# A new written order for the long convolution and the start of the MLP in a two-layer convolution and MLP kernel

## The chip, the cores and the metric

The kernel runs on one core of one Trainium2 chip. The metric is device time in microseconds (us), the median of three runs. A core has five engines that each take their own instructions in order and wait for each other through semaphores: TensorE (PE, matmuls), VectorE (DVE), ScalarE (ACT), GpSimd (POOL) and SyncE (SP, which here issues nearly all DMAs). DMAs are transfers between memory and on-chip SBUF, or within SBUF. Matmuls write PSUM, from which DVE or ACT copies the result to SBUF.

## The reference, cut to what matters

```python
x = A_q
x = x + A(LN(x), k, v, shift_k, ssm_k, ssm_D)
x = x + B(LN(x), w1, b1, w2, b2)
x = x + A(LN(x), k, v, shift_k, ssm_k, ssm_D)
x = x + B(LN(x), w1, b1, w2, b2)

def A(q, k, v, ...):            # S = 2048 tokens, D = 512 channels
    kv = shift(k, 4 taps) * v
    y = irfft(rfft(kv padded) * rfft(ssm_k padded))[:S] + kv * ssm_D
    return q * y
def B(x, w1, b1, w2, b2):       # F = 1376
    return gelu(LN(x) @ w1 + b1) @ w2 + b2
```

The result y of the convolution depends on k, v and the filters alone, so it is computed once and used in both layers.

## The kernel before: tiles, stages and what sets the order

The convolution is a two-stage transform, all of it matmuls with tables. Channels go in four chunks of 128 (cc 0 to 3), the 32 outer frequencies in four groups of eight (j 0 to 3). Every bit of work is a named **piece**:

- `lk`, `lv`, `lK`, `lx0`, `lF`, `lW`, `lM` are loads (k, v, the filter ssm_k in four quarters, the first tokens of q, tables). `kT` transposes k, `kv` is the 4-tap shift as matmuls (L513), `kvm` multiplies it by v on DVE out of PSUM (L521). The last chunk's taps run on POOL (`kg`, `ka`, `kgm`, L445 to L456).
- `KS` and `K2` transform the filter (L384, L394). `sa`, `sb` are eight DMAs that write its real and imaginary halves swapped (L401).
- `U..S`, `U..T` are the first stage for the signal (L302, L334 or a transposing DMA, L281).
- `X{cc}{j}` is the second stage, eight matmuls of 128 columns (L548), copied from PSUM to a buffer `xb`. `T{cc}{j}` multiplies it with the filter's spectrum, both operands in SBUF (L563), by DVE or by POOL. `V{cc}{j}` is the way back, 16 matmuls (L571), copied from PSUM to a buffer `ZT`. `T33` and `V33` come in two halves, a and b.
- `Z{cc}{g}` are transposing DMAs for chunks 0 to 2 (L619), `TD{g}` are transposes of chunk 3 on PE (L607), `Y{g}` is the last matmul stage for a group of four token tiles (L639).
- `s00`, `s01`, `s02` are the layer norm of the first tokens. `g0`, `h0`, `p0`, `b0`, `LT` are the gate, the statistics, the norm and the transposes of the first token group, `M` the first product of its MLP (L695) with its gelu (L703). `w1` to `w4` load the MLP's weights. `wm` are matmuls whose results nobody reads.

Nothing decides the order at run time or by a planner. A long string `ORDER` (L18) is written out by hand as words such as `T00.G` or `X01.P21`: the piece, a letter for the engine (P, D for DVE, A for ACT, G for POOL, S for SP) and the numbers of the buffers that it takes (`P` alone: which of four PSUM buffers; for X the second number is the `xb` buffer, of nine; three `ZT` buffers in the same way). `write` (L91 to L100) emits the pieces in just this order, under manual scheduling, so each engine gets its words in the string's order. For an evacuation of PSUM the letter chooses ACT or DVE (L208), for a `T` piece DVE or POOL (L559).

After the string the program continues in plain loops: second product of the MLP for the first group (L766), then seven more groups (L732, L766), with the second layer's norm and gate between them.

Of the kernel before, what the change touches and what calls it, by code (L numbers as in the profile page):

```python
# [15 lines left out]


ORDER = """  # L18
lk0.S lSK.S wm0.P0 bS.P2 bSK.P1 lk1.S bSe.A lb1.S kT1.P0 lF.S kT0.P2 bB.P3 dg1.D dg0.D kT0e.D bSKe.A kT1e.A lh1.S kT3.P1 kT2.P0 lh113.S dg2.A lv0.S kv01.P2 bBe.D kT3e.D lK11.S kvm01.D lv1.S kv00.P1 lK01.S kv20.P2 kvm00.D lK10.S kvm20.D kd6.P1 kT2e.A U1S0.P00 U1S0e.D kv02.P3 kd6e.A KS71.P2 KS71e.A KS70.P1 KS61.P0 lK00.S KS70e.A kvm02.D U1S1.P3 KS61e.D U1S1e.D kv03.P2 kd2.P0 U0S0.P11 kd2e.A U0S0e.A kvm03.D KS60.P3 U0S2.P0 U0S2e.A KS60e.D U2S0.P22 KS21.P1 kd4.P3 kd4e.D U0S3.P0 U2S0e.A U0S3e.A KS51.P3 KS40.P2 KS40e.A KS21e.D KS51e.D KS20.P1 KS30.P0 wm1.P2 KS30e.A KS20e.D U2S1.P3 U2S1e.A KS50.P2 kd0.P0 kd0e.D KS31.P1 KS50e.A KS00.P0 KS00e.A KS31e.D KS01.P3 KS11.P2 KS41.P1 KS10.P0 lx0.S KS01e.D KS11e.A U1S2.P3 U0S1.P2 KS41e.D KS10e.A kg0.G kg1.G ka1.G kg2.G ka2.G kg3.G ka3.G U0S1e.A wm2.P1 U1S2e.D lH.S lW.S K24.P0 K24e.A K23.P1 K23e.A K29.P2 K27.P3 K27e.A K29e.A kv21.P0 K21.P1 s00.D kvm21.D K22.P3 K20.P2 K21e.A K22e.D K26.P0 K25.P1 K25e.D K20e.A K28.P3 K211.P2 K211e.D K26e.A K210.P0 K28e.A U2S2.P1 lM.S K210e.A K213.P3 K213e.A U2S2e.D K214.P2 K212.P0 K212e.D s01.G kgm.G K214e.A K215.P1 sa0.S K215e.A U0T0.P3 U0T0e.D U1S3.P2 sb0.S U2S3.P0 U1S3e.A U0T1.P1 X00.P30 X01.P21 U2S3e.A X00e.A T00.G U0T1e.D X01e.A U2T0.P0 U3S0.P11 U3S0e.A U2T1.P3 U3S3.P2 U3S3e.A U2T0e.D X20.P02 X20e.A T20.G U2T1e.D U3S1.P1 U3S1e.D U3S2.P3 U1T0.P2 X23.P00 sa2.S U1T1.P1 sb1.S U1T0e.D U3S2e.A U1T1e.D sa3.S X11.P33 X23e.A X22.P24 sa1.S sb3.S X11e.A X21.P05 X21e.A sb2.S U3T0.S lx.S U3T1.S X03.P16 X22e.D X03e.A T23.D ly.S X12.P37 X02.P22 X13.P08 X12e.A V00.P1 T21.D X10.P30 X13e.A V20.P00 X02e.A V00e.A X10e.A T01.D T22.D V23.P2 V20e.A V22.P1 V22e.A T03.D V03.P3 V03e.A V23e.A V21.P0 T02.D T10.D V02.P1 V01.P3 V02e.A V21e.D T12.D T13.D V01e.A Z21.S Z20.S X30.P00 X32.P22 X32e.A X30e.D V10.P11 V13.P3 V10e.A V13e.A X31.P28 X31e.A V12.P0 T11.D Z00.S Z01.S T30.D T32.D V11.P1 V12e.A T31.D V11e.A X33.P33 Z22.S Z10.S Z11.S V30.P22 V32.P0 X33e.A w1.S V32e.A T33a.D T33b.D V30e.A V31.P1 V31e.D V33a.P3 V33ae.A V33b.P0 V33be.A TD0a.P1 TD0ae.A s02.D TD0b.P3 TD0be.D Y00.P0 Y00e.A Y01.P1 TD3.P3 g00.D h00.D p00.G Z02.S Y01e.A TD1.P2 TD2.P0 TD3e.A TD1e.A TD2e.A Y02.P3 g01.D Y10.P2 b00.D LT0.P1 Y02e.A LT0e.A Z12.S Y12.P0 h01.D p01.G g02.D Y10e.A Y12e.A M0b.P3 M0be.A M0a.P1 b01.D h02.D LT1.P0 M0ae.A LT1e.D Z03.S Y20.P3 M1b.P0 p02.G b02.D LT2.P2 M1be.A LT2e.A M1a.P1 M2a.P0 Y20e.A M1ae.A M2ae.A M2c.P3 M2ce.A M2b.P2 M2be.A Y22.P0 w3.S w4.S Z13.S Z23.S Y32.P3 Y30.P1 LG1.D Y32e.A w2.S Y30e.A Y22e.A
"""  # L20
NA, NB = 32, 64

# [824 lines left out]
```

## Time and profile before

| what | us |
|---|---|
| median of three runs | 248.03 |
| lowest and highest run | 246.64, 249.02 |
| span of the profiled execution, first to last instruction | 245.9 |
| PE busy | 236.2 |
| DVE busy | 169.9 |
| ACT busy | 137.0 |
| POOL busy | 62.5 |

The page gives no time of the profiled execution but its span; the span lies 2.1 us below the median of the runs and 0.7 us below the lowest. Times in views are us from the start of the span. In a timeline a row has start, length, engine, line, operation, output and input, and a count; in the chain of waits a row has start, length and what the chain went through. "SPq" is the SP queue issuing a DMA. The convolution and the MLP's begin take the span's first 99.7 us; from there the seven regular steps take 19.0 us each.

### The profile page before, as it was taken

How to read it: one execution, taken by the hardware profiler on the slowest of the kernel's cores; microseconds unless marked ns; L12 is line 12 of the kernel's file. 1: busy time of each engine (PE TensorE's matmuls, PEld its weight loads, DVE VectorE, ACT ScalarE, POOL GpSimd, SP SyncE). 2: the span in 40 equal slices, each digit the busy share in tenths (PEclk: the TensorE clock that was granted, in tenths of full speed). 3: DMA queues.
4: the chain of work that ended last, by engine and by line, in shares of the span. 5: the costliest groups of instructions: out<-in, count | busy, mean ns of one | idle time of the engine just before them, and what ended most of it. 6: DMA issues, size and time to landing. Idle time of an engine off the chain costs nothing.

```text
span 245.9 us, 4897 instructions
## 1 busy us (share of the span) xinstructions
PE 236.2 (96%) x1989; PEld 142.5 (58%) x2002; DVE 169.9 (69%) x325; ACT 137.0 (56%) x197; POOL 62.5 (25%) x51
## 2 busy tenths in 40 slices
PE   6999999999997899999999999999999999999994
PEld 2898874898896588444444444444444444444443
DVE  0579799689998997878899898857956951021022
ACT  2706999989998989507307406506505604704700
POOL 2399999584000211111101111101011010000000
PEclk9999999999999999999999999999999999999999
DMA  6999907999999997040402104012025015011011
GB/s 248 346 259 185 287 16 248 356 387 223 306 173 183 255 159 235 3 87 0 85 0 53 36 0 85 3 35 51 1 58 115 0 43 128 3 43 43 0 42 43
DMA packets 56431, 29.64 MB, mean 121 GB/s; under 512 B 48883, under 2 KB 52696, under 8 KB 55514
## 3 DMA queue, kind: packets, MB, share of 16 engines
q1 hardware_dynamic: 56402, 29.34, 48.2%
q8 instruction: 15, 0.25, 0.4%
q14 instruction: 6, 0.05, 0.1%
q10 hardware_dynamic: 8, 0.00, 0.0%
HBM read 15.18 MB, written 2.10 MB: 70 GB/s over the span
## 4 chain that ended last, share of the span: by engine, by line
PE 81%; DVE 7%; ACT 3%; DMA 3%; issue 2%; SPq 1%; POOL 1%; DVEq 0%; POOLq 0%
PE po L766 31%; PE ph L732 27%; PE p L513 4%; PE p L695 4%; DVE arena L212 4%; DMA arena<-in_B_w_dram 3%; PE p L571 3%; PE p L412 2%; DVE arena L563 2%; PE p L334 2%; PE p L302 2%; ACT ZT L210 2%; PE p L384 1%; PE p L431 1%; PE p L548 1%
## 5 line engine op out<-in xcount | busy, mean ns | idle before, releaser
L734 ACT ACTIVATE arena<-ph,B 128x512 bf16<-128x512 f32 (+1 forms) x77 | 52.8, 687 | 79.1 <-PE ph L732 78.9
L766 PE MATMUL po<-arena 128*128 128x512 bf16 (+3 forms) x355 | 77.0, 372 | 0.4
L732 PE MATMUL ph<-arena 128*128 128x512 bf16 (+1 forms) x308 | 67.6, 379 | 0.0
L766 PEld LDWEIGHTS <-arena 128*128 128x128 bf16 (+1 forms) x363 | 35.5, 98 | 40.7
L771 DVE TENSOR_TENSOR arena<-po,arena 128x512 bf16<-128x512 f32 (+1 forms) x33 | 21.5, 672 | 44.5 <-PE po L766 44.5
L732 PEld LDWEIGHTS <-arena 128*128 128x128 bf16 (+1 forms) x308 | 30.8, 100 | 35.9
L210 ACT ACTIVATE arena<-p 128x1024 bf16<-128x1024 f32 (+6 forms) x43 | 38.8, 990 | 9.1 <-PE p L378 5.3
L248 POOL TENSOR_TENSOR lrsm<-lrsm,mhalf 128x4 f32<-128x4 f32 (+2 forms) x10 | 9.3, 927 | 78.8 <-DVE lrsm L242 78.8
L210 ACT ACTIVATE ZT<-p 128x1024 bf16<-128x1024 f32 (+1 forms) x22 | 21.0, 1006 | 0.9 <-PE p L302 0.4
L232 DVE BATCH_NORM_STATS2 lstm<-arena 128x6 f32<-128x512 bf16 x32 | 20.0, 681 | 0.2
L232 DVE BATCH_NORM_STATS2 lstg<-arena 128x6 f32<-128x512 bf16 x32 | 19.7, 678 | 0.0
L248 POOL TENSOR_TENSOR lrsg<-lrsg,mhalf 128x4 f32<-128x4 f32 x8 | 8.1, 1011 | 44.5 <-DVE lrsg L245 44.5
L563 DVE TENSOR_TENSOR arena<-xb,arena 128x2048 bf16<-128x2048 bf16 (+1 forms) x15 | 16.9, 1181 | 0.2 <-ACT xb L210 0.2
L571 PE MATMUL p<-arena 128*128 128x128 bf16 x256 | 16.2, 219 | 0.8 <-ACT xb L210 0.3
L253 DVE TENSOR_SCALAR arena<-arena,lmvg,lrsg 128x512 bf16<-128x512 bf16 x32 | 11.0, 409 | 7.9 <-POOL lrsg L248 7.9
L445 POOL TENSOR_TENSOR arena<-arena,SK 128x2048 bf16<-128x2048 bf16 (+3 forms) x4 | 14.9, 3750 | 3.6 <-ACT DG L423 3.4
L571 PEld LDWEIGHTS <-arena 128*128 128x128 bf16 x256 | 14.6, 98 | 2.1 <-DVE arena L563 1.2
L212 DVE CAST arena<-p 128x1024 bf16<-128x1024 f32 (+1 forms) x14 | 14.6, 1088 | 1.6 <-ACT arena L210 0.7
L210 ACT ACTIVATE xb<-p 128x1024 bf16<-128x1024 f32 x14 | 13.8, 1040 | 0.7 <-PE p L548 0.5
L253 DVE TENSOR_SCALAR arena<-arena,lmvm,lrsm 128x512 bf16<-128x512 bf16 x32 | 11.4, 413 | 2.2 <-POOL lrsm L248 2.2
L212 DVE COPY arena<-p 128x2048 bf16<-128x2048 bf16 (+3 forms) x10 | 10.2, 1025 | 3.5 <-PE p L334 1.4
L452 POOL TENSOR_TENSOR arena<-arena 128x2048 bf16<-128x2048 bf16 x3 | 12.2, 4066 | 0.2
(74 smaller groups left out, 231.5 us busy)
## 6 DMA issues: line engine op xcount, KB each, us to landing
arena<-arena SPq DMA_DIRECT2D x8, 512.0 KB, 8.7
arena<-in_A_k_dram SPq DMA_DIRECT2D x2, 1024.0 KB, 6.3
arena<-in_A_v_dram SPq DMA_DIRECT2D x2, 1024.0 KB
arena<-in_A_ssm_k_dram SPq DMA_DIRECT2D x4, 512.0 KB, 7.1
arena<-tabM SPq DMA_DIRECT2D x1, 2048.0 KB, 9.3
out_dram<-arena SPq DMA_DIRECT2D x15, 128.0 KB, 1.7
arena<-in_A_q_dram SPq DMA_DIRECT2D x1, 1536.0 KB, 6.8
arena<-in_B_w_dram SPq DMA_DIRECT2D x1, 1376.0 KB, 8.0
```

The lines of the kernel that those rows point to most:

```text
L210: nc.scalar.activation(dst, src, AF.Copy)
L212: nc.vector.tensor_copy(dst, src)
L232: nc.vector.bn_stats(self.st[:, i, 0, :], x_t[:, GT * g + i, :] if src is None else src[:, i, :])
L248: nc.gpsimd.tensor_tensor(self.rs[:, a:b], self.rs[:, a:b], mhalf[:, a:b], ALU.pow)
L253: nc.vector.tensor_scalar(out=dst[:, i, :], in0=xs, scalar1=self.mv[:, i, 0:1], scalar2=self.rs[:, i:i + 1], op0=ALU.subtract, op1=ALU.mult)
L445: nc.gpsimd.tensor_tensor(m[:, t:NT, :], kn[:, 0:NT - t, c3], sk(t, NT - t), ALU.mult)
L563: eng.tensor_tensor(kk, x2, kk, ALU.mult)
L571: nc.tensor.matmul(o[:, i, :], spec[:, cc, ka + i, :], Mt[:, ka + i, r, :], start=r == 0, stop=r == 1)
L732: nc.tensor.matmul(o.rearrange("p (i t) -> p i t", t=P), W1t[:, ct, ft * P:ft * P + m], lt[:, a:b, ct, :], start=ct == 0, stop=ct == CT - 1)
L734: nc.scalar.activation(hT[0:m, ft, a * P:b * P], o, AF.Gelu_apprx_tanh, bias=B1[0:m, ft:ft + 1])
L766: nc.tensor.matmul(po[:, a:b], hT[0:m, ft, i * P:(i + 1) * P], W2t[0:m, ft, a:b], start=ft == 0, stop=ft == FT - 1)
L771: nc.vector.tensor_tensor(xs, po[:, a:b], xs, ALU.add)
```

## The change

The string `ORDER` is replaced as a whole; no other line changes. It has the same pieces. What differs is their order on every engine, the PSUM, `xb` and `ZT` buffers, and for a number of evacuations and products the engine. A program can't be read from these words, so of the diff stand here only the lines' beginnings:

```diff
 ORDER = """
-lk0.S lSK.S wm0.P0 bS.P2 bSK.P1 lk1.S bSe.A lb1.S kT1.P0 lF.S kT0.P2
...
+wm0.P0 lk0.S lSK.S bS.P3 bSe.D dg1.D lb1.S lh113.S lF.S lk1.S kT0.P1
...
 """
```

**The products on POOL and DVE.** On POOL, after the last product of the shift (L456), stand the products with the filter's spectrum (L563; `xb` is the second stage's result). As a piece of the difference:

```order
 L456 TENSOR_TENSOR arena<-arena 128x16x128
 L563 TENSOR_TENSOR arena<-xb_95,arena 128x2x1024
-L563 TENSOR_TENSOR arena<-xb_97,arena 128x2x1024
+L563 TENSOR_TENSOR arena<-xb_96,arena 128x2x1024
+L563 TENSOR_TENSOR arena<-xb_100,arena 128x2x1024
+L563 TENSOR_TENSOR arena<-xb_98,arena 128x2x1024
+L563 TENSOR_TENSOR arena<-xb_95,arena 128x2x1024
+L563 TENSOR_TENSOR arena<-xb_102,arena 128x2x512 x2
 L248 TENSOR_TENSOR lrsm_112<-lrsm_112,mhalf 128x1 x2
```

POOL had two of these products (T00, T20). It now has five whole ones and both halves of a sixth: T10, T00, T01, T03, T21, T33a, T33b, in this order.

On DVE, at the same place, stood before:

```order
L212 CAST xb_99<-p_121 128x1024
L563 TENSOR_TENSOR arena<-xb_95,arena 128x2x1024
L563 TENSOR_TENSOR arena<-xb_100,arena 128x2x1024
L563 TENSOR_TENSOR arena<-xb_96,arena 128x2x1024
L563 TENSOR_TENSOR arena<-xb_99,arena 128x2x1024
L563 TENSOR_TENSOR arena<-xb_101,arena 128x2x1024
L563 TENSOR_TENSOR arena<-xb_97,arena 128x2x1024
L563 TENSOR_TENSOR arena<-xb_95,arena 128x2x1024
L212 CAST ZT_92<-p_119 128x32x32
```

and stands now:

```order
L563 TENSOR_TENSOR arena<-xb_97,arena 128x2x1024
L212 COPY arena<-p_122 128x16x128
L563 TENSOR_TENSOR arena<-xb_101,arena 128x2x1024
L563 TENSOR_TENSOR arena<-xb_99,arena 128x2x1024
L212 CAST xb_103<-p_119 128x1024
L563 TENSOR_TENSOR arena<-xb_102,arena 128x2x1024
L212 CAST ZT_94<-p_120 128x32x32
L212 CAST xb_97<-p_121 128x1024
L563 TENSOR_TENSOR arena<-xb_103,arena 128x2x1024
L212 CAST xb_99<-p_121 128x1024
L563 TENSOR_TENSOR arena<-xb_97,arena 128x2x1024
L563 TENSOR_TENSOR arena<-xb_96,arena 128x2x1024
```

The rows now are T12, a copy of U2T0, T13, T11, a copy of X20, T02, copies of V13 and X23, T20, a copy of X30, T23 and T22; behind them follow T30, T31, a copy of V22 and T32. DVE had thirteen whole products and two halves and has ten whole ones; between them it now has six copies out of PSUM (the L212 rows and that of V22) where there were two.

**The weight load on SP.** The transposing DMAs (Z, L619) and the first MLP weight w1 (`in_B_w`, 128x4x1376) on SP, as a piece of the difference:

```order
-L619 DMA_TRANSPOSE arena<-ZT_92 128x8x128 x2
+L619 DMA_TRANSPOSE arena<-ZT_94 128x8x128 x3
 L619 DMA_TRANSPOSE arena<-arena 128x8x128 x2
-L619 DMA_TRANSPOSE arena<-ZT_92 128x8x128
 L619 DMA_TRANSPOSE arena<-ZT_93 128x8x128 x2
 L278 DMA arena<-in_B_w_dram 128x4x1376
```

Seven Z stand ahead of w1 in both. Before they were Z21, Z20, Z00, Z01, Z22, Z10, Z11; now they are Z11, Z10, Z13, Z03, Z00, Z20, Z23, so that the ones just before w1 read chunk 2, whose last V piece on PE is now V21, behind T20, T22, T23 and T21.

**The early loads on SP.** The second half of v, three quarters of the filter, the first tokens of q, and the table GP, as a piece of the difference:

```order
 L278 DMA arena<-in_A_v_dram 128x4096
 L345 DMA arena<-in_A_ssm_k_dram 128x32x64
+L278 DMA GPt<-tabGP 128x256
+L345 DMA arena<-in_A_ssm_k_dram 128x32x64
+L278 DMA arena<-in_A_q_dram 128x2048
 L278 DMA arena<-in_A_v_dram 128x4096
-L345 DMA arena<-in_A_ssm_k_dram 128x32x64 x3
-L278 DMA arena<-in_A_q_dram 128x2048
-L278 DMA GPt<-tabGP 128x256
+L345 DMA arena<-in_A_ssm_k_dram 128x32x64 x2
 L278 DMA Wt<-tabW 128x4096
```

The second half of v is now behind two quarters of the filter and the first tokens of q; before it was behind one quarter. With q's load the statistics s00 on DVE moved too: they stood behind the filter's copies and stand now ahead of kvm03, kvm21 and kvm02. The second half of k went behind three small loads (b1, the last rows of k's halo, the table F).

On PE the same matmuls stand in another order. Of the filter's K2 pieces, K20 to K23, which the first swap DMA reads, are now among the first five and were among the first seven; one kv piece went from between the K2 pieces to ahead of them, and two `wm` of one matmul each from ahead of them to behind V33. In the V pieces the chunks' order was 0, 2, then 1, 3, and is now 1, 0, then 2, 3. Of the Y pieces, Y30 and Y32 went ahead of the first M and Y10 and Y12 behind it. The loops behind the string are the same.

More of the change, by code (lines that the diff above doesn't have):

```diff
@@ L18 @@
 ORDER = """
-lk0.S lSK.S wm0.P0 bS.P2 bSK.P1 lk1.S bSe.A lb1.S kT1.P0 lF.S kT0.P2 bB.P3 dg1.D dg0.D kT0e.D bSKe.A kT1e.A lh1.S kT3.P1 kT2.P0 lh113.S dg2.A lv0.S kv01.P2 bBe.D kT3e.D lK11.S kvm01.D lv1.S kv00.P1 lK01.S kv20.P2 kvm00.D lK10.S kvm20.D kd6.P1 kT2e.A U1S0.P00 U1S0e.D kv02.P3 kd6e.A KS71.P2 KS71e.A KS70.P1 KS61.P0 lK00.S KS70e.A kvm02.D U1S1.P3 KS61e.D U1S1e.D kv03.P2 kd2.P0 U0S0.P11 kd2e.A U0S0e.A kvm03.D KS60.P3 U0S2.P0 U0S2e.A KS60e.D U2S0.P22 KS21.P1 kd4.P3 kd4e.D U0S3.P0 U2S0e.A U0S3e.A KS51.P3 KS40.P2 KS40e.A KS21e.D KS51e.D KS20.P1 KS30.P0 wm1.P2 KS30e.A KS20e.D U2S1.P3 U2S1e.A KS50.P2 kd0.P0 kd0e.D KS31.P1 KS50e.A KS00.P0 KS00e.A KS31e.D KS01.P3 KS11.P2 KS41.P1 KS10.P0 lx0.S KS01e.D KS11e.A U1S2.P3 U0S1.P2 KS41e.D KS10e.A kg0.G kg1.G ka1.G kg2.G ka2.G kg3.G ka3.G U0S1e.A wm2.P1 U1S2e.D lH.S lW.S K24.P0 K24e.A K23.P1 K23e.A K29.P2 K27.P3 K27e.A K29e.A kv21.P0 K21.P1 s00.D kvm21.D K22.P3 K20.P2 K21e.A K22e.D K26.P0 K25.P1 K25e.D K20e.A K28.P3 K211.P2 K211e.D K26e.A K210.P0 K28e.A U2S2.P1 lM.S K210e.A K213.P3 K213e.A U2S2e.D K214.P2 K212.P0 K212e.D s01.G kgm.G K214e.A K215.P1 sa0.S K215e.A U0T0.P3 U0T0e.D U1S3.P2 sb0.S U2S3.P0 U1S3e.A U0T1.P1 X00.P30 X01.P21 U2S3e.A X00e.A T00.G U0T1e.D X01e.A U2T0.P0 U3S0.P11 U3S0e.A U2T1.P3 U3S3.P2 U3S3e.A U2T0e.D X20.P02 X20e.A T20.G U2T1e.D U3S1.P1 U3S1e.D U3S2.P3 U1T0.P2 X23.P00 sa2.S U1T1.P1 sb1.S U1T0e.D U3S2e.A U1T1e.D sa3.S X11.P33 X23e.A X22.P24 sa1.S sb3.S X11e.A X21.P05 X21e.A sb2.S U3T0.S lx.S U3T1.S X03.P16 X22e.D X03e.A T23.D ly.S X12.P37 X02.P22 X13.P08 X12e.A V00.P1 T21.D X10.P30 X13e.A V20.P00 X02e.A V00e.A X10e.A T01.D T22.D V23.P2 V20e.A V22.P1 V22e.A T03.D V03.P3 V03e.A V23e.A V21.P0 T02.D T10.D V02.P1 V01.P3 V02e.A V21e.D T12.D T13.D V01e.A Z21.S Z20.S X30.P00 X32.P22 X32e.A X30e.D V10.P11 V13.P3 V10e.A V13e.A X31.P28 X31e.A V12.P0 T11.D Z00.S Z01.S T30.D T32.D V11.P1 V12e.A T31.D V11e.A X33.P33 Z22.S Z10.S Z11.S V30.P22 V32.P0 X33e.A w1.S V32e.A T33a.D T33b.D V30e.A V31.P1 V31e.D V33a.P3 V33ae.A V33b.P0 V33be.A TD0a.P1 TD0ae.A s02.D TD0b.P3 TD0be.D Y00.P0 Y00e.A Y01.P1 TD3.P3 g00.D h00.D p00.G Z02.S Y01e.A TD1.P2 TD2.P0 TD3e.A TD1e.A TD2e.A Y02.P3 g01.D Y10.P2 b00.D LT0.P1 Y02e.A LT0e.A Z12.S Y12.P0 h01.D p01.G g02.D Y10e.A Y12e.A M0b.P3 M0be.A M0a.P1 b01.D h02.D LT1.P0 M0ae.A LT1e.D Z03.S Y20.P3 M1b.P0 p02.G b02.D LT2.P2 M1be.A LT2e.A M1a.P1 M2a.P0 Y20e.A M1ae.A M2ae.A M2c.P3 M2ce.A M2b.P2 M2be.A Y22.P0 w3.S w4.S Z13.S Z23.S Y32.P3 Y30.P1 LG1.D Y32e.A w2.S Y30e.A Y22e.A
@@ new lines @@
+wm0.P0 lk0.S lSK.S bS.P3 bSe.D dg1.D lb1.S lh113.S lF.S lk1.S kT0.P1 bB.P2 bBe.D lh1.S dg0.D kT1.P0 lv0.S kT1e.D kT0e.A kT3.P3 bSK.P2 kT2.P1 lK10.S bSKe.A kv01.P0 kg0.G kg1.G kT3e.D kT2e.D dg2.A kvm01.D kv00.P2 lH.S lK00.S kv20.P3 kd4.P1 kvm00.D kd4e.D U1S0.P00 lx0.S lv1.S kvm20.D KS51.P2 U1S0e.A lK11.S KS41.P1 KS51e.A U2S0.P31 lK01.S KS50.P0 KS41e.D KS50e.A KS40.P2 kv03.P1 KS40e.A kd0.P0 U2S0e.D kv21.P3 s00.D kvm03.D U0S0.P22 kd0e.A U0S0e.A kv02.P0 kvm21.D KS10.P2 KS00.P1 kvm02.D KS10e.A KS01.P3 kd6.P0 KS11.P2 KS00e.A kd6e.D KS61.P0 U1S3.P1 KS01e.D KS71.P3 ka1.G KS61e.D KS11e.A kg2.G U1S3e.A KS60.P2 KS71e.D kd2.P0 U1S1.P1 kd2e.A U1S1e.D U0S3.P0 KS30.P3 KS60e.A lW.S lM.S ka2.G KS31.P2 KS30e.D U0S3e.A KS31e.A KS21.P1 KS20.P0 KS70.P3 KS20e.D U0S1.P2 KS21e.A U0S1e.D U2S1.P1 U1S2.P0 KS70e.A K23.P3 U2S1e.A K20.P2 K23e.D K27.P1 U1S2e.A K22.P0 K20e.A K21.P3 K25.P2 K27e.D K21e.D K22e.A K26.P1 s01.G K24.P0 K215.P3 K25e.A K26e.D K24e.A U0S2.P2 K213.P1 kg3.G K215e.D U0S2e.A K213e.A K211.P0 K214.P2 K212.P3 K211e.D K212e.D K214e.A K28.P1 U1T0.P0 ka3.G K29.P2 kgm.G K28e.A sa0.S K210.P3 U1T1.P1 U1T0e.D K29e.A K210e.A U2S2.P2 U2S2e.A U1T1e.D U3S0.P00 s02.D U0T0.P3 X10.P10 sb0.S sa1.S U3S2.P2 U3S0e.A U0T1.P0 X10e.A sb1.S sa3.S U0T0e.D U0T1e.D U3S2e.A U3S1.P1 X00.P31 U3S3.P2 X00e.D U3S1e.A T10.G U3S3e.A X12.P02 sb2.S X12e.A U2S3.P1 X03.P33 U2S3e.D X11.P24 X01.P05 X03e.A X01e.A sb3.S X13.P16 T00.G U2T0.P3 X13e.A sa2.S X02.P07 X11e.D U2T1.P2 T12.D U2T0e.D X02e.A V10.P12 X20.P08 T13.D U2T1e.A V12.P3 V10e.A V00.P2 V13.P1 V12e.A T11.D V00e.A U3T0.S X20e.D T02.D ly.S X21.P00 V11.P3 U3T1.S lx.S V13e.D X21e.A V11e.A Z11.S X23.P22 X22.P01 T01.G X31.P16 X23e.D Z10.S T03.G V02.P3 X22e.A X31e.A X30.P24 V02e.A T20.D X30e.D V01.P0 T23.D T21.G V01e.A X33.P17 T22.D X32.P35 V03.P2 T30.D X33e.A V03e.A X32e.A T31.D V20.P01 V22.P1 V22e.D V23.P2 V21.P3 Z13.S T32.D V20e.A V30.P00 Z03.S T33a.G Z00.S V23e.A V31.P2 V21e.A V30e.A Z20.S Z23.S w1.S T33b.G V31e.D V32.P1 V33a.P3 Z01.S Z21.S V33b.P0 V32e.A V33be.A wm2.P2 wm1.P1 V33ae.D TD0a.P2 TD0b.P3 Z12.S TD0ae.D Y00.P1 TD0be.D Y00e.A TD3.P0 TD3e.A Y01.P2 Y02.P3 TD2.P0 g00.D w4.S h00.D Z02.S p00.G Y30.P1 Y01e.A Y02e.A Y32.P3 g01.D TD2e.A TD1.P0 b00.D h01.D p01.G g02.D LT0.P2 b01.D Y30e.A LT0e.A M0a.P1 h02.D LT1.P2 Y32e.A Z22.S M0b.P3 LT1e.D TD1e.A M0ae.A p02.G M0be.A Y10.P0 Y10e.A M1a.P2 b02.D LG1.D LT2.P1 Y12.P3 LT2e.A M1b.P0 M1ae.A w2.S Y12e.D M2b.P1 Y20.P3 M1be.A M2c.P2 M2a.P0 M2be.A M2ce.A Y22.P1 Y20e.A w3.S M2ae.A Y22e.A
```

## Prediction

> **What bounds the kernel now.** I read the page first, to see which engine carries the span.
>
> ```profile
> PE 236.2 (96%) x1989; PEld 142.5 (58%) x2002; DVE 169.9 (69%) x325; ACT 137.0 (56%) x197; POOL 62.5 (25%) x51
> PE 81%; DVE 7%; ACT 3%; DMA 3%; issue 2%; SPq 1%; POOL 1%; DVEq 0%; POOLq 0%
> ```
>
> PE does, so an order can gain only what PE waits, about 10 us in all (245.9 - 236.2), and can lose without limit. Next the chain in order of time, where the changed stretch ends.
>
> ```profile
> 59.01 2.22 DVE arena L563 x2
> ...
> 70.87 1.82 PE p L571 x32
> ...
> 76.08 1.34 SPq L619
> ...
> 77.59 7.99 DMA arena<-in_B_w_dram
> 85.58 0.05 issue
> 85.62 2.64 PE p L695 x44
> ...
> 97.53 2.32 PE p L639 x10
> 99.85 8.43 PE po L766 x39
> ```
>
> Before 77 us the chain alternates between PE and DVE's products (L563); then SP issues the Z transposes, then the weight w1, which takes 7.99 us, and the first M waits for it until 85.62. Behind that point the new order has the same work: the M pieces, LT1, LT2 and four Y (before Y20, Y22, Y32, Y30, now Y10, Y12, Y20, Y22), then loops that did not change. So **the change is worth what it moves 85.62**.
>
> **Two engines, one way into SBUF.** The largest edit gives POOL five and a half products instead of two, at a time when DVE has products too. The rows by line show what each costs, and one that stands out.
>
> ```profile
> L563 DVE TENSOR_TENSOR arena<-xb,arena x4: 1210/1211/1825, 57.3 to 61.3; 128x2048 bf16<-128x2048 bf16 x4
> ...
> L563 DVE TENSOR_TENSOR arena<-xb,arena x12: 684/1209/1211, 61.3 to 75.8; 128x2048 bf16<-128x2048 bf16 x10, 128x1024 bf16<-128x1024 bf16 x2
> ...
> L563 POOL TENSOR_TENSOR arena<-xb,arena x2: 4078/4090/4102, 49.9 to 53.9; 128x2048 bf16<-128x2048 bf16 x2
> ...
> 53.92 4.08 POOL L563 TENSOR_TENSOR arena<-xb,arena 128x2048 bf16<-128x2048 bf16 x1
> ```
>
> Of thirteen whole DVE products twelve took 1.21 us (start to start 1.14) and one 1.825. That one is the first, at 57.26, and it alone met a POOL product, which ended at 53.92 + 4.08 = 58.00. It ended at 57.26 + 1.825 = 59.09, which is 1.09 after POOL: of the 0.74 us in common, DVE lost 0.62, nearly all. The other direction is there too:
>
> ```profile
> 82.44 0.58 POOL L248 TENSOR_TENSOR lrsm<-lrsm,mhalf 128x1 f32<-128x1 f32 x1 [24.44 <-DVE lrsm L242]
> 84.83 0.94 POOL L248 TENSOR_TENSOR lrsm<-lrsm,mhalf 128x1 f32<-128x1 f32 x1 [1.80 <-DVE lrsm L242]
> ...
> 82.28 0.68 DVE L666 TENSOR_TENSOR arena<-arena,p 128x512 bf16<-128x512 bf16 x1
> ...
> 84.67 0.68 DVE L666 TENSOR_TENSOR arena<-arena 128x1024 bf16<-128x1024 bf16 x1
> ```
>
> The same tiny POOL instruction took 0.58 us under a DVE product with one operand in PSUM (p), and 0.94 when started under one with both in SBUF. DVE work out of PSUM does not suffer: three casts beside POOL's L452 keep their pace of 1.1 to 1.2 us.
>
> ```profile
> 28.00 4.07 POOL L452 TENSOR_TENSOR arena<-arena 128x2048 bf16<-128x2048 bf16 x1
> ...
> 30.09 3.49 DVE L212 CAST arena<-p 128x1024 bf16<-128x1024 f32 x3 [0.21 <-PE p L384]
> ```
>
> I conclude that a DVE product with two SBUF operands and a POOL product exclude each other, each for its whole length. The trace before hides this, since its two POOL products lie before DVE's first but for 0.74 us.
>
> The Trainium skill says so against this change (SBUF — State Buffer, "Who interferes with whom"): a VectorE instruction with two SBUF inputs contends with a GpSimd instruction that reads SBUF, and whichever issues first holds the shared port while the other blocks fully. By that rule the trace agrees, 1.825 against 1.21 us. Were it a sharing of bandwidth instead, the sum would be that of the rivals near no change below.
>
> **The sum.** (1) *Where POOL starts.* Its first product waited for the swap DMAs, the first of them issued at 40.16, behind K2 (L394).
>
> ```profile
> 49.85 8.15 POOL L563 TENSOR_TENSOR arena<-xb,arena 128x2048 bf16<-128x2048 bf16 x2 [3.18 <-DMA arena<-arena]
> ...
> 13.20 8.99 SPq L345 DMA_DIRECT2D arena<-in_A_ssm_k_dram  x3
> ...
> 34.63 2.46 DVE L232 BATCH_NORM_STATS2 lstg<-arena 128x6 f32<-128x512 bf16 x4
> 37.01 0.36 DVE L236 BATCH_NORM_AGGREGATE lmvg<-lstg 128x2 f32<-128x6 f32 x4
> ...
> 34.28 1.46 PE p L394 x6
> 35.73 1.80 PE p L513 x32
> ...
> 40.16 10.12 SPq L278 DMA_DIRECT2D arena<-arena  x8
> ...
> arena<-arena SPq DMA_DIRECT2D x8, 512.0 KB, 8.7
> ```
>
> Two K2 pieces fewer (two matmuls each; six took 1.46, so about 0.5 a piece) and one kv piece (1.80) less between K2's start and the first swap: -2.8. The same kv piece stands ahead of K2 now, +1.8, and two single warming matmuls don't, -0.8 (0.38 each, the shortest L412 below). Against that the early loads: the statistics (2.46 + 0.36 = 2.8) now hold up three kvm, which free PSUM, and wait for q behind two filter quarters; k's second half is later by three small loads. No row shows these waits. They lie between 0 (PE has other pieces meanwhile) and 5.8 us (all of 2.8, and one more filter quarter ahead of q at 8.99 / 3 = 3.0); I take 2.4, nearer to the statistics' row, since that wait stands on DVE for certain. Together +0.6: POOL starts at 50.5.
>
> (2) *The two in turn*, 4.1 for POOL's, 1.1 for DVE's, the one that asked first going first (no row shows which does; the bounds have the other way). POOL T10 50.5 to 54.6, T00 to 58.7. DVE's T12 needs the last swap, which was issued 1.3 before the eight's end at 50.28 and lands by the page's median 8.7 later, near 58; it gets 58.7 to 59.8. POOL T01 to 63.9, DVE T13 to 65.0, POOL T03 to 69.1, DVE T11 to 70.2, the copy of X20 to 71.3 and T02 to 72.4. Here is a hole of 0.5: POOL's T21 needs X21, whose PSUM buffer is free only with X20's copy, so T21 runs 72.9 to 77.0. DVE T20 to 78.1, POOL T33a (half, 2.05) to 80.1, DVE T23 to 81.2, POOL T33b to 83.2, DVE T22 to 84.3. Check by the plain sum from T00's start: POOL 4 x 4.1 + 2 x 2.05 = 20.5, DVE seven x 1.14 = 8.0, hole and copies 1.2, together 54.6 + 29.7 = 84.3. While DVE stands still so do the copies behind it, so PE has no free PSUM buffer and waits.
>
> (3) *From T22 to M.*
>
> ```profile
> L210 ACT ACTIVATE ZT<-p 128x1024 bf16<-128x1024 f32 (+1 forms) x11 | 10.1, 987 | 0.1
> ...
> 73.33 4.09 SPq L619 DMA_TRANSPOSE arena<-ZT  x3
> ...
> 78.02 0.71 PE L607 MATMUL p<-IDt,ZT 128*128 128x128 bf16 x8 [0.87 <-ACT ZT L210]
> ...
> 83.80 0.40 PE L647 MATMUL p<-IDt,arena 128*128 128x128 bf16 x4 [0.21 <-DVE arena L253]
> ```
>
> V22, V23, V21 on PE 3 x 0.91 (two took 1.82), V21's copy on ACT 1.0: 88.0. Only then can Z20 and Z23 go, 1.36 each on SP (three took 4.09), and w1 stands behind them: issued 90.8, landed 7.99 later, 98.8. A second path meets it: V30 to V33 end at 87.0 + 4 x 0.91 + two warming matmuls, near 91; before, V33 ended 0.87 before 78.02 and the first tokens' gate, norm and LT0 (L647, then its copy, 0.4) were there at 84.6, 7.4 later; so now near 98.6. Either way M starts at 98.8 instead of 85.62: **+13.2**. The span becomes 259.1; with the 2.1 us by which the median of runs lies above this span, **261 us**.
>
> **Bounds.** If exclusion is as the row has it but DVE goes first whenever two of its products follow each other, POOL's T03 and T33b come later and PE waits less: -2. The early waits give -2.4 to +3.4, one for one. Holes where neither runs, +3. So 255 to 267 for this case.
>
> **The rivals.** *Free products, PE better fed (not slower).* If both engines run side by side, DVE sheds three whole and two half products, 3 x 1.14 + 2 x 0.6 = 4.6 us, in a stretch where PE waits for them:
>
> ```profile
> PEld L571 <- DVE arena L563: 1.2, 4, 0.4
> ...
> PE p L571 <- DVE arena L563: 0.3, 1, 0.3
> ```
>
> That is 1.5 us to win, and with 0.5 lost early the time is 247. It decides where a DVE product beside POOL's is stretched by less than 0.2 us (1.5 over the seven ahead of V22), 1.4 us in all; against it stands the one row of 1.825. *Free products, early loss kept:* the 2.4 of step (1) reach V21, thus w1, and nothing gives them back: 250, +0.8%. For it speaks that w1 is behind V21 on either path, against it the same row. *Exclusion and a slow clock:* in the layout PE waits 4 to 5 us at a time around T03 and T11, and the trace shows slow matmuls where PE came from rest:
>
> ```profile
> L412 PE MATMUL p<-IDt x15: 376/631/631, 2.1 to 33.6; 128*128 128x512 bf16 x15
> ...
> 2.08 4.94 PE p L412 x13
> ```
>
> Thirteen took 4.94, 0.38 each, where L766's 39 take 8.43, 0.22 each. If that happens again at one restart that nothing covers, some 4 us of matmuls take twice as long or half again, +3.5 on the forecast: 264.5. Against it: PE is short of work there anyway. The Trainium skill has a rule for it (TensorE: Matmul & The Clock Gate, "What's actually happening"): an idle window of about 3.4 us halves the clock until as long a busy one; no idle stretch of that length after the start is in this trace.
>
> **How the numbers follow.** Exclusion as summed 0.68; with a slow clock 0.10; free with early loss 0.12; free and better fed 0.10. A measurement of this kernel tells about 1%, 2.5 us, from no change. Both exclusion cases are slower beyond that (0.78); of 250 a quarter (0.03), the rest the same (0.09); of 247 four in ten faster (0.04), the rest the same (0.06). Faster 0.04, same 0.15, slower 0.81. The forecast is 261; its own range 255 to 267. Since 0.22 lies on the rivals near no change, the range reaches down over 250 to 248, and up to 267.
>
> **What would show it.** Right: DVE L563 rows of 3 to 5 us, each ending 1.1 us after a POOL L563 row; POOL's L563 beyond 4.1 where it started under DVE; PE idle for several us at L571 and L548 between 58 and 85 by "DVE arena L212" and L563; w1 issued near 91, not 77.6; the regular steps still 19.0 us. Wrong in (2): DVE L563 at 1.2 us beside a running POOL L563; then a rival holds. Wrong in (1): K2 starting before 35 or after 39. Wrong in (3): w1 issued early while M waits for LT0 alone. A granted clock below 1.0 between 70 and 95 would speak for the third rival.

## The result, and the profile after

The changed kernel takes **262.94 us** (median of 6 runs, 262.16 to 264.12), the kernel before 247.66 (6 runs): 1.0618 times as long, with a 95% interval of 1.0586 to 1.065. The profiled execution took 262.38 us with a span of 260.7, against a span of 245.9 before. The forecast was 261.0 us.

The page's engines and its PE slices:

```profile
PE 239.8 (92%) x1989; PEld 146.1 (56%) x2002; DVE 185.8 (71%) x328; ACT 132.8 (51%) x189; POOL 81.8 (31%) x56
PE   6999799996396798999999999999999999999995
PEclk9999999998759999999999999999999999999999
```

PE is busy for only 3.6 us more, in a span that is 14.8 longer: it waits for the rest. The slices of 6.5 us show where: a 7 near 29 us, then a 6 and a 3 from 59 to 72, a 6 and a 7 from 78 to 91 and an 8 behind 98; the rest is 9, but for the first and the last. DVE is busy for 15.9 us more with three instructions more, so its instructions became longer. The rows of the product line L563 say which:

```profile
L563 DVE TENSOR_TENSOR arena<-xb,arena x10: 1207/2836/5066, 57.0 to 90.2; 128x2048 bf16<-128x2048 bf16 x10
...
L563 POOL TENSOR_TENSOR arena<-xb,arena x7: 2208/4071/5044, 51.9 to 83.8; 128x2048 bf16<-128x2048 bf16 x5, 128x1024 bf16<-128x1024 bf16 x2
```

DVE's product had a median of 1209 ns before; now it is 2836, and the longest takes 5066. How they come to it is seen one by one in the timeline, start and length in us, first DVE's T12, T13 and T11:

```profile
57.03 4.09 DVE L563 TENSOR_TENSOR arena<-xb,arena 128x2048 bf16<-128x2048 bf16 x1
62.17 3.94 DVE L563 TENSOR_TENSOR arena<-xb,arena 128x2048 bf16<-128x2048 bf16 x1
66.04 5.07 DVE L563 TENSOR_TENSOR arena<-xb,arena 128x2048 bf16<-128x2048 bf16 x1
```

and POOL's T00, T01 and T03 beside them:

```profile
55.92 4.11 POOL L563 TENSOR_TENSOR arena<-xb,arena 128x2048 bf16<-128x2048 bf16 x1
59.99 5.04 POOL L563 TENSOR_TENSOR arena<-xb,arena 128x2048 bf16<-128x2048 bf16 x1
65.00 5.03 POOL L563 TENSOR_TENSOR arena<-xb,arena 128x2048 bf16<-128x2048 bf16 x1
```

Add start and length. POOL's T00 ends at 60.03 and DVE's T12 at 61.12; T01 ends at 65.03, T13 at 66.11; T03 at 70.03, T11 at 71.11. Each DVE product ends 1.08 to 1.09 us after POOL's, about one DVE product's own time (1.14 from start to start), and T01 and T03 are 1 us longer than 4.1, the time of the DVE product that was ahead of them. They take turns, and PE pays:

```profile
62.31 0.62 PE L548 MATMUL p<-arena,Wt 128*128 128x128 bf16 x8 [2.24 <-DVE arena L212]
...
72.29 1.01 PE L548 MATMUL p<-arena,Wt 128*128 128x128 bf16 x8 [4.77 <-DVE xb L212]
...
85.02 2.85 PE L571 MATMUL p<-arena 128*128 128x128 bf16 x48 [2.25 <-DVE arena L563]
...
91.48 1.96 PE L571 MATMUL p<-arena 128*128 128x128 bf16 x32 [1.20 <-DVE arena L563]
```

These four waits come to 10.5 us. The end of the stretch by the chain of waits, to be read against 76.08, 77.59 and 85.62 of before:

```profile
89.16 1.13 DVE ZT L212
90.29 1.15 DVE arena L563
...
91.48 1.53 PE p L571 x24
...
93.08 7.92 DMA arena<-in_B_w_dram
...
101.04 1.96 PE p L695 x32
...
115.05 3.24 PE po L766 x15
```

The weight w1 is issued at 93.08 instead of 77.59 and M starts at 101.04 instead of 85.62, 15.4 later, of which the end keeps 14.8. The chain puts w1 behind 24 matmuls of V32 and V33a (L571), whose end at 93.01 falls together with w1's turn; but in the order w1 stands ahead of both, and what it stood behind are two Z on SP (step (3) below). The start of M in each run carries the rest of this text: before 85.62, after 101.04, and four more in the experiments.

### The profile page after: what moved, and what is told of

The parts are those of the page before. It is cut to its first block, busy times and chain, and to the rows that moved or that the text cites. A ratio compares the mean times of both kernels' runs of the same rounds, so it can differ in the third digit from the quotient of the medians.

```text
span 260.7 us, 4900 instructions
## 1 busy us (share of the span) xinstructions
PE 239.8 (92%) x1989; PEld 146.1 (56%) x2002; DVE 185.8 (71%) x328; ACT 132.8 (51%) x189; POOL 81.8 (31%) x56
## 4 chain that ended last, share of the span: by engine, by line
PE 60%; DMA 3%; DVE 1%; issue 0%; SPq 0%
PE po L766 29%; PE ph L732 26%; PE p L695 4%; DMA arena<-in_B_w_dram 3%; PE p L639 1%; PE p L571 1%; DVE arena L563 0%; DVE ZT L212 0%; PE p L647 0%; DVE arena L771 0%; SPq L278 0%
## 5 line engine op out<-in xcount | busy, mean ns | idle before, releaser
L210 ACT ACTIVATE arena<-p 128x1024 bf16<-128x1024 f32 (+6 forms) x40 | 37.7, 995 | 11.5 <-PE p L431 4.6
L563 POOL TENSOR_TENSOR arena<-xb,arena 128x2048 bf16<-128x2048 bf16 (+1 forms) x7 | 27.4, 3944 | 12.2 <-ACT xb L210 12.2
L563 DVE TENSOR_TENSOR arena<-xb,arena 128x2048 bf16<-128x2048 bf16 x10 | 26.4, 2674 | 0.0
L571 PE MATMUL p<-arena 128*128 128x128 bf16 x256 | 18.4, 235 | 4.4 <-DVE arena L563 3.8
L232 DVE BATCH_NORM_STATS2 lstg<-arena 128x6 f32<-128x512 bf16 x32 | 19.7, 680 | 2.2 <-DMA arena<-in_A_q_dram 2.2
L571 PEld LDWEIGHTS <-arena 128*128 128x128 bf16 x256 | 16.7, 106 | 5.5 <-DVE arena L563 5.1
L212 DVE CAST arena<-p 128x1024 bf16<-128x1024 f32 (+1 forms) x16 | 16.9, 1106 | 1.3 <-PE p L378 0.9
L548 PE MATMUL p<-arena,Wt 128*128 128x128 bf16 x128 | 10.3, 240 | 7.2 <-DVE xb L212 4.8
L210 ACT ACTIVATE xb<-p 128x1024 bf16<-128x1024 f32 x11 | 10.7, 1032 | 7.2 <-DVE arena L563 6.5
L548 PEld LDWEIGHTS <-Wt 128*128 128x128 bf16 x128 | 9.1, 110 | 7.8 <-issue 5.4
```

Of the source, the lines that this page charges most:

```text
L210: nc.scalar.activation(dst, src, AF.Copy)
L212: nc.vector.tensor_copy(dst, src)
L232: nc.vector.bn_stats(self.st[:, i, 0, :], x_t[:, GT * g + i, :] if src is None else src[:, i, :])
L548: nc.tensor.matmul(o[:, i, :], Wt[:, k0 + i, :], chunk(ZX, cc)[:, k0 + i, :], start=True, stop=True)
L563: eng.tensor_tensor(kk, x2, kk, ALU.mult)
L571: nc.tensor.matmul(o[:, i, :], spec[:, cc, ka + i, :], Mt[:, ka + i, r, :], start=r == 0, stop=r == 1)
```

## The experiments

In the shorthand of the diffs, words of the order that did not change are left out.

**One product on POOL.** The changed order, all but T10 moved back to DVE.

```diff
-T10.G T00.G T01.G T03.G T21.G T33a.G T33b.G
+T10.G T00.D T01.D T03.D T21.D T33a.D T33b.D
```

> The changed order with one thing undone: T00, T01, T03, T21, T33a and T33b go from POOL to DVE, only T10 stays on POOL (it lies ahead of DVE's first product). Exclusion (mine): the 14.7 us by which DVE's products were stretched and the 3 us of POOL's own waiting vanish, and DVE gets 4 x 1.14 + 2 x 0.6 = 5.8 us of products back; every DVE product at 1.2 us, w1 issued near 81 instead of 93, time 250 to 255 us. What is left above 247.7 is the early part and the order. Rival, the order and the early loads do it, POOL's products are free help: losing POOL's help makes it no faster, 262 us or more.

251.8 us, 1.0171 times before (1.0142 to 1.0199). Taking POOL's help away made the changed order 11 us faster, and every DVE product is short again:

```profile
L563 DVE TENSOR_TENSOR arena<-xb,arena x16: 684/1216/1219, 56.2 to 80.6; 128x2048 bf16<-128x2048 bf16 x14, 128x1024 bf16<-128x1024 bf16 x2
```

The start of M, and K2's row by its source line, here and in the kernel before:

```profile
90.30 1.95 PE L695 MATMUL p<-arena 128*128 128x128 bf16 x32 [0.69 <-ACT arena L210]
```

```profile
L394 PE MATMUL p<-arena,Wt x30: 376/377/379, 37.9 to 47.1; 128*128 128x512 bf16 x30
```

```profile
L394 PE MATMUL p<-arena,Wt x30: 376/378/379, 33.8 to 43.8; 128*128 128x512 bf16 x30
```

M is still 4.7 late, and K2 4.0 (its first matmul started at 33.85 before). M's last wait is now for a copy by ACT (by the order that of LT0, the second path of step (3)) and no longer for w1. So POOL's products bring most of the loss, and something else the rest.

**POOL busy without reading.** Is it that POOL works, or that it reads SBUF? Each POOL product became a copy of one column and two memsets of the region that it wrote.

```diff
-eng.tensor_tensor(kk, x2, kk, ALU.mult)
+if it["eng"] == "G":
+    eng.tensor_copy(one column of kk, one column of xb)
+    for _ in range(2):
+        eng.memset(kk, 0.0)
+    return
+eng.tensor_tensor(kk, x2, kk, ALU.mult)
```

> The changed kernel with POOL kept as busy, at the same places in its queue, but without reading SBUF: in place of each POOL product stand a copy of one column and two memsets of the same region (so the products T10, T00, T01, T03, T21, T33a, T33b are left out of the result, the region is zero instead). Exclusion by what both engines read (mine): DVE's products go back to 1.2 us beside a running POOL, time 246 to 253 us, and this is also what the change would have cost had products been free. Rival, any POOL work that writes SBUF stretches DVE: DVE products of 3 to 5 us as before, time 258 to 263.

247.9 us, 1.0002 times before (0.9979 to 1.0024). By the source lines (DVE's product is L568 here, POOL's copy L564):

```profile
L568 DVE TENSOR_TENSOR arena<-xb,arena x10: 1211/1216/1219, 57.2 to 74.2; 128x2048 bf16<-128x2048 bf16 x10
...
L566 POOL MEMSET arena<- x14: 952/1805/1806, 52.3 to 76.6; 128x2048 bf16 x10, 128x1024 bf16 x4
...
L564 POOL COPY arena<-xb x7: 187/189/1150, 52.0 to 75.2; 128x1 bf16<-128x1 bf16 x7
```

POOL is kept busy from 52 to 77 us, and no DVE product is longer than 1.22. The memsets, which only write, neither wait nor make wait; the one-column copies, which read, took up to 1.15 us instead of 0.19 where a DVE product was running. A pair of memsets with its copy is 0.2 us shorter than a product (3.67 + 0.19 against 4.07), too little for 15. M starts nearly where it did before:

```profile
86.50 1.95 PE L700 MATMUL p<-arena 128*128 128x128 bf16 x32 [0.69 <-ACT arena L210]
```

So **the loss of the change, 15 us, is the exclusion**: it goes when POOL no longer reads. Without it the new order would be worth what the old one is.

**POOL reading one operand.** Each POOL product became the chunk of x times 1.0, written to the same place.

```diff
+if it["eng"] == "G":
+    eng.tensor_scalar(kk, x2, 1.0, None, ALU.mult)
+    return
 eng.tensor_tensor(kk, x2, kk, ALU.mult)
```

> The changed kernel with each POOL product replaced by one POOL instruction that reads one SBUF operand in place of two (the chunk of x times 1.0, written to the same place; so the filter's factor is left out of those seven products). Exclusion, if one operand read by POOL is enough (mine): each DVE product that meets it still ends about 1.1 us after it, and POOL's waits for a running DVE product; with an instruction of 2 to 4 us the time lies at 252 to 262, and the DVE rows tell. Rival, only two operands on both sides exclude each other: DVE's products stay at 1.2 us beside a running POOL, time 246 to 253 whatever POOL's length.

258.14 us, 1.0415 (1.0369 to 1.046). One such instruction and the DVE product that met it:

```profile
62.73 5.38 POOL L564 TENSOR_SCALAR arena<-xb 128x2048 bf16<-128x2048 bf16 x1
```

```profile
63.17 4.27 DVE L566 TENSOR_TENSOR arena<-xb,arena 128x2048 bf16<-128x2048 bf16 x1
```

One operand is enough to exclude. But the expectation "ends 1.1 us after it" failed: DVE ended at 67.44, before POOL's 68.11. With 1.14 us of its own it began to run near 66.3, which is 3.6 into POOL's 5.38; the other products blocked by a whole instruction of this kind give 3.6 as well. By the records this instruction lets go before its end; a POOL record is rough, so the 3.6 is an estimate. Why it takes longer than the product with two operands stays open.

**DVE reading one operand.** The other side: POOL's products stay, each of DVE's ten became x times 1.0.

```diff
+if it["eng"] == "D":
+    eng.tensor_scalar(kk, x2, 1.0, None, ALU.mult)
+    return
 eng.tensor_tensor(kk, x2, kk, ALU.mult)
```

> The changed kernel with POOL's products as they are, and each of DVE's ten replaced by one DVE instruction with a single SBUF operand (x times 1.0, written to the same place; so the filter's factor is left out of those ten). Two SBUF operands on DVE are needed for the exclusion (mine, from the trace): DVE's instruction keeps its own length, 0.6 to 1.2 us, beside a running POOL product, POOL's at 4.1, time 245 to 251. Rival, DVE's quick single-operand form takes the same way into SBUF as POOL: rows of 3 to 5 us that end right behind POOL's, time 255 to 262.

257.3 us, 1.0388 (1.0334 to 1.0442): my theory fell here, the rival held. DVE's rows, one blocked and one alone, and POOL's beside the first:

```profile
65.39 4.54 DVE L564 TENSOR_SCALAR arena<-xb 128x2048 bf16<-128x2048 bf16 x1
...
70.98 0.68 DVE L564 TENSOR_SCALAR arena<-xb 128x2048 bf16<-128x2048 bf16 x1
```

```profile
64.88 4.50 POOL L566 TENSOR_TENSOR arena<-xb,arena 128x2048 bf16<-128x2048 bf16 x1
```

Alone it takes 0.68; beside POOL 4.54, and it ends at 69.93, 0.55 after POOL's 69.38. An instruction with a single SBUF operand is held just as long. It is shorter than the product, which fits that less is lost in all; that link was not tried by itself.

**The engines alone, in the order before.** The kernel before with the change's engines for T, then the same with memsets on POOL.

```diff
-T00.G T20.G T10.D T01.D T03.D T21.D T33a.D T33b.D
+T00.G T20.D T10.G T01.G T03.G T21.G T33a.G T33b.G
```

> The kernel before, its order kept, with the change's choice of engines alone: T10, T00, T01, T03, T21, T33a and T33b on POOL, T20 on DVE. Exclusion (mine): DVE's products are stretched to 3 to 5 us in this order too, time 258 to 266, so the engines alone bring the whole loss. Rival, products run side by side and the order does it: DVE rows at 1.2 us; between 248 (POOL's slower products hidden) and 255 (POOL's six late products in a row, 5 x 4.1, end behind the place where V wants them).

> The order before with the change's choice of engines, as in the run with these engines alone, which took 267.4 us, but each of the seven POOL products replaced by the copy of one column and two memsets of the same region (those products are left out of the result). Exclusion (mine): the loss of 19.7 us was DVE's and POOL's waiting for each other and the slow matmuls behind it, so it goes: DVE's products at 1.2 us and a time of 246 to 254, where what is left above 247.7 is POOL's slower pace (3.9 us a piece). Rival, in this order the products come too late because POOL is slow, exclusion or not: 258 or more.

267.39 us, 1.0782 (1.0737 to 1.0828), and with memsets 264.33, 1.0668 (1.0597 to 1.0739). The first number, 1.4 above my range, seemed to fit my theory, and the second took it away: without exclusion nearly all of the loss is still there, 16.9 of 19.7 us. With memsets no DVE product is stretched; PE waits for POOL instead:

```profile
73.17 5.60 PE L576 MATMUL p<-arena 128*128 128x128 bf16 x64 [6.90 <-POOL arena L566]
```

and DVE for PE:

```profile
76.88 1.23 DVE L212 CAST ZT<-p 128x1024 bf16<-128x1024 f32 x1 [11.41 <-PE p L576]
```

In that order T21, T01, T03 and T10 stand one behind the other in POOL's queue, 3.9 us each from 60.6 to 77, and V03, early on PE, waits 6.90 us for T03. The new order has T10 and T00 first on POOL and V03 late, so the same pieces came in time there. This pair says little for the exclusion, 3 us between the two; a cleaner one was wanted.

**One word.** The kernel before with T11 alone on POOL, where POOL is idle; then with memsets in POOL's three products.

```diff
-T11.D
+T11.G
```

> The kernel before, one word of its order changed: the product T11 runs on POOL instead of DVE, in the middle of DVE's products, when POOL has nothing else to do. Exclusion (mine): DVE stands still for POOL's 4.1 us and is spared 1.14, so V, w1 and M go some 3 us later (a little more where POOL waits for DVE first): 250 to 252.5, and one or two DVE products of 3 to 5 us around it. Rival, an idle engine takes a product off the busy one and it costs nothing: 246 to 248.5.

> The same with POOL's product T11 replaced by a copy of one column and two memsets of its region (the product is left out of the result). Exclusion by what POOL reads (mine): DVE's products stay at 1.2 us and DVE is spared one, 246 to 248. Rival, T11 comes too late on the slower engine whatever the port (as the pair of runs with all seven in this order had it, 267.4 and 264.3): 250 or more, like the run with the product itself.

252.04 us, 1.017 (1.012 to 1.022), against 247.28, 0.9954 (0.9931 to 0.9977). The one product and its neighbour on DVE:

```profile
57.06 5.06 POOL L563 TENSOR_TENSOR arena<-xb,arena 128x2048 bf16<-128x2048 bf16 x1
```

```profile
58.12 5.08 DVE L563 TENSOR_TENSOR arena<-xb,arena 128x2048 bf16<-128x2048 bf16 x1
```

POOL waited 1.0 us for DVE's first product, then DVE waited for the 4.1 us of POOL's, until 62.12, and ended at 63.20. DVE's first seven products, with the product and with memsets:

```profile
56.72 12.15 DVE L563 TENSOR_TENSOR arena<-xb,arena 128x2048 bf16<-128x2048 bf16 x7
```

```profile
57.56 8.03 DVE L568 TENSOR_TENSOR arena<-xb,arena 128x2048 bf16<-128x2048 bf16 x7
```

That is 4.1 us more. In this order too the exclusion costs 4 to 5 us for one product more (a little of it is T20's, as in the trace before), and a POOL that did not read would bring 1.

**Three on POOL.** The changed order with T10, T00 and T01 on POOL.

```diff
-T03.G T21.G T33a.G T33b.G
+T03.D T21.D T33a.D T33b.D
```

> The changed order with three products on POOL (T10, T00, T01), the others on DVE; the run with T10 alone took 251.8, the change with five and a half 262.9. Exclusion, each product moved to POOL costs its 4.1 us less the 1.14 that DVE saves, in so far as it lies beside DVE's products: T00 lies half ahead of DVE's first (1.5), T01 wholly beside (up to 3): 254 to 256.5. Rival, the loss sits in one hole, the 4.8 us in which PE waits for X20's copy behind T03: with T03 back on DVE the time stays within 1 us of 251.8.

255.7 us, 1.0325 (1.0256 to 1.0393), 4 above the run with T10 alone (1.0171). In the profiled execution, a short one of 254.28 us, M starts near 93.0. The time grows with the products moved, 251.8, 255.7 and 262.9 with one, three and five and a half; it does not sit in one hole.

**The early part alone.** The kernel before with the norm of the first tokens put ahead, as the change has it.

```diff
-lK10.S kvm20.D ... kvm03.D ... lx0.S ... kv21.P0 K21.P1 s00.D
+lK10.S lx0.S kvm20.D ... kvm03.D s00.D ... kv21.P0 K21.P1
```

> The early part alone, on the kernel before: the statistics and the norm of x (s00) stand on DVE right behind the third filter mask (kvm03) instead of behind kv21, and its load (lx0) one place further ahead on SP; nothing else moves. My step (1), an early wait goes one for one into the end: the regular pieces K2 start near 37.5 instead of 33.85, first swap, w1 and M go along, time 250 to 252.5. Rival, the early loss is given back since PE and DVE have slack behind it (as the kernel with memsets on POOL hints, whose K2 began at 37.7 too and which took 247.9): 247 to 249.

254.37 us, 1.0276 (1.0227 to 1.0324), above my 252.5. K2's row by its source line, two rows of PE ahead of it, and the start of M:

```profile
L394 PE MATMUL p<-arena,Wt x30: 376/377/379, 41.4 to 51.3; 128*128 128x512 bf16 x30
```

```profile
30.39 0.21 PE L377 MATMUL p<-arena,IDt 128*128 128x32 bf16 x1 [5.59 <-DVE arena L212]
...
31.42 3.62 PE L384 MATMUL p<-Ft,arena 128*64 128x128 bf16 x64
...
93.13 2.63 PE L695 MATMUL p<-arena 128*128 128x128 bf16 x44 [0.64 <-DMA arena<-in_B_w_dram]
```

K2 starts 7.5 later than its 33.85 of before and M 7.5 later than 85.62: one for one, as step (1) had it. My size for the delay, 3.7, was half of what it was, since the statistics stand on DVE waiting for q's load, the copies out of PSUM queue behind them, and PE stood still for 5.59 us. Most of the rest is the clock: from 30 to 36 us the granted clock was 0.50, and the 64 matmuls of L384 there took 3.62 us, where 64 of them took 2.06 before.

## Why the prediction was right

**What bounds.** "Worth what it moves 85.62" held: M moved by 15.4, the span by 14.8.

**Step (1), where POOL starts: right in sign, too small.** The early waits were taken as 2.4 and POOL's start as 50.5.

```profile
23.14 2.47 DVE L232 BATCH_NORM_STATS2 lstg<-arena 128x6 f32<-128x512 bf16 x4 [2.21 <-DMA arena<-in_A_q_dram]
```

```profile
37.63 0.38 PE L394 MATMUL p<-arena,Wt 128*128 128x512 bf16 x1
```

```profile
51.90 18.12 POOL L563 TENSOR_TENSOR arena<-xb,arena 128x2048 bf16<-128x2048 bf16 x4 [4.63 <-ACT xb L210]
```

DVE waited 2.21 us for q; K2 came at 37.63 (the step's terms make 37.25), the first swap at 41.94 instead of 40.76, and POOL's T10 at 51.90. It no longer waited for the swaps, as in the trace before, but for ACT's copy of X10. So POOL started 1.4 later than predicted, within the bound of 3.4 above the value taken, but by another wait than the one in the sum. That the 2.4 came out near is luck in part: it was a choice between 0 and 5.8, and s00 put ahead in the old order costs 7.5.

**Step (2), the two in turn: right, product by product.** T12, T01, T13, T03 and T11 came in the predicted order, 0.9 to 1.3 us behind the predicted times, which is the 1.4 of step (1). From there the holes were larger. T21 ended at 78.55 (predicted 77.0), and T33a, predicted from 78.1, started at 81.67:

```profile
81.67 5.27 POOL L563 TENSOR_TENSOR arena<-xb,arena 128x1024 bf16<-128x1024 bf16 x2 [3.12 <-ACT xb L210]
```

POOL waited 3.12 us for X33's copy. T22 still ended at 84.96, against 84.3, since T23 went ahead of T33a and T22 ahead of T33b; T33b then met T30, which moved the price to the next step. Two sums of the prediction do not close: "hole and copies 1.2" in its check is 0.5 + 1.1 in its layout, and 261 less 2 less 2.4 is 256.6, where it put 255 as the lower end of its own range. Neither touches the outcome.

**Step (3), from T22 to M: the size was 1.6 too small, and the piece that decides was another.** It named V21's copy on ACT, at 88.0, 3.7 behind T22. That is the second of two copies here, and ended at 88.95, 4.0 behind T22:

```profile
87.01 1.94 ACT L210 ACTIVATE ZT<-p 128x1024 bf16<-128x1024 f32 x2 [2.25 <-PE p L571]
```

But what SP waited for last is in its list of waits (in all, times, longest):

```profile
SPq L619 <- DVE ZT L212: 4.7, 1, 4.7
```

```profile
90.36 2.61 SPq L619 DMA_TRANSPOSE arena<-ZT  x2
```

It waited for the copy of V22 on DVE, which ended at 90.29, 5.3 behind T22. It stands behind T30 and T31, and T30 was held by T33b:

```profile
83.84 3.10 POOL L563 TENSOR_TENSOR arena<-xb,arena 128x1024 bf16<-128x1024 bf16 x1
```

```profile
84.88 3.14 DVE L563 TENSOR_TENSOR arena<-xb,arena 128x2048 bf16<-128x2048 bf16 x1
...
89.08 1.21 DVE L212 CAST ZT<-p 128x1024 bf16<-128x1024 f32 x1
```

So two Z transposes (until 92.97) and w1 followed from 90.3 instead of 88.0: of the 2.2 by which M came later than 98.8, 0.7 was there at T22 and 1.6 was added here. Behind M the change was 0.6 shorter than before, and the span ended 1.6 above the predicted 259.1. An engine that is made to wait delays every instruction behind it in its queue; the sum had counted the products and not all the copies between them.

**The rule: right for this kernel, too narrow as I put it.** I concluded "a DVE product with two SBUF operands and a POOL product exclude each other". For two products the whole-length exclusion stands, and which comes first is settled by who asked first: with T11 alone moved, POOL asked at 57.06 and went ahead of DVE's product that asked at 58.12. The two operands do not matter: one on POOL is enough, and so is one on DVE in its quick form. The Trainium skill has this better (SBUF — State Buffer, "SBUF: two separate sides"): it counts a VectorE instruction in a two-port mode among those that take the shared pair, and names two SBUF inputs as contending only with a GpSimd instruction that reads SBUF. The trace agrees on both points: 4.54 against 0.68 us for the quick form, 1.22 at most beside memsets. That it holds for the whole length was not seen with POOL's single-operand form, which let go after 3.6 of its recorded 5.38 us.

**The rivals.** "Free products, PE better fed" gave 247 for a chip without exclusion; the memsets on POOL are that case, and took 247.9. Its inner sum can now be seen in the starts of M. Before 85.62; with T10 alone on POOL 90.30, 4.7 later, of which K2's start explains 4.0 if it goes one for one as in the early part alone; with free POOL work 86.50, so free help gives back 3.8; with real products 101.04, so exclusion costs 14.5. The two rivals near no change each had one of the two halves.

**The slow clock** of the third rival did happen. Time in the window, PE's busy time, and further right the granted clock, DMA share and GB/s:

```profile
63.50:66.50 3.00, 2.62 (x26) 2.35 (x24) 3.00 (x2) 1.65 (x2) 3.00 (x2) 0.50 1.13 258
66.50:70.20 3.70, 1.03 (x15) 0.91 (x14) 3.70 (x1) 0.40 (x1) 3.52 (x1) 0.96 0.30 102
70.20:77.00 6.80, 4.71 (x45) 4.71 (x45) 5.35 (x5) 2.23 (x3) 2.51 (x1) 0.50 0.00 0
77.00:95.00 18.00, 13.85 (x217) 12.24 (x215) 16.63 (x13) 11.92 (x13) 6.82 (x3) 1.00 0.57 107
```

From 70.2 to 77 the clock was 0.50, and the eight X matmuls behind PE's wait of 4.77 us took 1.01 us instead of 0.62. The Trainium skill's rule (TensorE: Matmul & The Clock Gate, "What's actually happening") has an idle window of about 3.4 us halve the clock. The trace agrees that half the clock comes with long waits, but not on the length: the clock fell some 2.7 us into that wait, and it was also 0.50 from 63.5 to 66.5, behind a wait of only 2.24 us.

What it cost in the end was not tried by itself. T21 waited for a copy behind those eight matmuls, so 0.4 us by the rows is likely on its path. More can be: PE worked without a pause from 72.29 until X33's matmuls near 80, until 77 at half clock, and X33's copy is what T33a waited for. M came 2.2 later than forecast; 1.6 of it arose behind 85 us at full clock, but because T33a was late and T33b so met T30. How much of the 2.2 is the clock's stays open; the rival's price, 3.5 on top of the forecast, is more than all of it.

## What to carry to other kernels

Before an elementwise product goes to an idle GpSimd, see what VectorE does in the same microseconds: if it reads SBUF in a form that shares the way, the move costs GpSimd's time less VectorE's own, here 4.07 less 1.14, 2.9 us by the rows and 3.9 as measured for one product, and everything queued behind VectorE waits too. In these runs VectorE kept its pace beside GpSimd where it read from PSUM, or where GpSimd only wrote; whether a product pays there was not tried. And a run with the right number proves little: of two runs with all the products moved, the one that removed the suspected cause kept the loss.

## What the hardware showed that I had not expected

- GpSimd's memsets of 128 x 2048 run beside VectorE's products without a trace of contention (1.22 us at most), while a GpSimd copy of a single column takes up to 1.15 us instead of 0.19.
- VectorE's single-operand form of 128 x 2048 takes 0.68 us and is held like the product, to 4.54.
- GpSimd's single-operand form takes 5.38 us, longer than the 4.07 of its product with two operands, and by the records VectorE was let in after 3.6.
- The granted clock of TensorE fell to 0.50 for some 3 us, from 63.5 on, though the wait ahead of it was only 2.24 us long.
